# A gated local-attention kernel: another order for the first four tiles, two pairs of projection buffers, and other halves gated at the end

## The chip, the cores and the metric

The kernel runs on one core of a Trainium2 chip, in one launch. The metric is the device time of the launch in microseconds (us), the median of several runs. Five engines work side by side, each through its own queue in order: TensorE (PE, matrix products and transposes, with its weight loads listed as PEld), VectorE (DVE), ScalarE (ACT), GpSimd (POOL) and SyncE (SP), which here issues all DMA transfers. Where an engine needs what another one makes, it waits on a semaphore.

## The reference

`x` has 2048 rows (positions) of 640 numbers. It is normalised row by row; two branches start from the normalised rows, and the result is `x + s * g`:

```python
xn = _layernorm(x, axis=-1)                        # S = 2048 rows, D = 640
# branch A: 32 heads of 20, each position attends to 8 positions, 2 apart, backwards
qkv = xn @ wqkv                                    # D x 3D
logits = einsum(q, k at pos - 2*w for w in 0..7) * Dh ** -0.5    # masked before the start
s = (softmax(logits) applied to the gathered v) @ wo             # D x D
# branch B: bilinear feed-forward
g = silu(((xn @ w_gate) * (xn @ w_up)) @ w_down)   # D x 1536, D x 1536, 1536 x D
return x + s * g
```

## The kernel before

**Tiles.** The 2048 rows are cut into 16 tiles of 128. Tiles 0 to 7 hold the even positions, tiles 8 to 15 the odd ones, so that a neighbour two positions back lies in the same half. A tile is loaded (`load_x`, line 132), its mean and variance are taken on DVE (`moments`, L185 and L186), one over the root of the variance is formed by a square root on ACT (L191) and a few narrow DVE instructions (`rstd`, L194 to L206), and the tile is scaled in place by one DVE instruction (`apply`, L209). `norm` does the last two steps for `n` tiles.

**Products in three parts.** Each float32 factor is split into a rounded part `hi`, a copy made by ACT, and the remainder `lo`, a subtraction on DVE or POOL (`split`, L85 and L86). A product is then three matmuls: hi by hi, hi by lo and lo by hi, each over five blocks of 128 of the 640 columns (`KD = 5`), so 15 matmuls for one output.

**Transposes.** PE needs a tile with its columns on the partitions. `trans` (line 218) transposes the five blocks of tiles 0 to 7 on PE (L223) into two PSUM buffers of four blocks and one. ACT copies each buffer to the `hi` part (L224), and DVE subtracts to get the `lo` part (L225). Tiles 8 to 15 go through DVE's own transpose (`trans_odd`).

**Stages.** (1) The start, lines 628 to 704: loads, norms and transposes of the tiles, with the first products of the projection to q, k and v (`qkv`, line 281; group 0 of six groups of heads, 300 columns) and of the gate and up matrices (`gate_up`, `f` a block of 128 of the 1536 columns, `ch` a chunk of four tiles). (2) The bulk: for twelve units (a group of heads and a half of the positions) the projection, with the attention on DVE advanced a little at a time between products (`advance`), and the rest of the gate and up products. (3) The output projection of the 16 tiles (`out_proj`, line 469), stored to `s_scr`. (4) The down projection, 56 block products (`product`), whose results are gathered, sent through SiLU on ACT (L579) and gated and added (`gated`, L584 and L585) before the store.

**Order.** Everything is in the order in which the program text issues it, on each engine's queue (a manual schedule); a tile pool hands out buffers by tag in turn, and an instruction that takes a buffer waits until the last reader of that buffer is done. What matters for the change:

- `load_wq` loads the weights of group 0 in five slices of 128 rows, `split_wq` splits them (hi on ACT, lo on POOL); `load_wf` and `split_wf` do the same for a gate/up block. All of them use tag `wraw` with three buffers, so the fourth load waits until the first buffer has been split.
- A DMA takes one of eight semaphores in turn and, on SP, the DMA eight places further on waits for it to land.
- `gate_up_first` runs the gate and up products for the first two tiles alone (256 of 512 columns), and `gate_up(0, 0, part=part0)` finishes the other two.
- PSUM tag `q` has four buffers, shared by transposes, `qkv`, `idle_product` (products of the identity with itself, whose result is not used) and the output projection.
- `out_proj` writes each tile to a buffer of tag `gs` (two buffers) by two ACT copies (L476) and stores it from there.
- `halves` holds the subtractions that `trans_odd` has put off; `low_parts` issues them.

The start, as issued before:

```python
norm(0, 1)
mv1 = moments(1, 1)
split_wq(0, nc.gpsimd, (0, 3))
trans(0)
idle_product()
split_wq(0, nc.gpsimd, (3, KD))
load_x(12, 1, xa[:, 0:1])
norm(1, 1, mv1)
begin_unit(0, False)
mv2 = moments(2, 2)
qkv(0, 0, ((0, 0), (1, 0), (0, 1)))
trans(1)
```

Of the kernel before, what the change touches and what calls it, by code (L numbers as in the profile page):

```python
# [19 lines left out]
P = 128  # L20
# [30 lines left out]
def kernel(  # L51
# [48 lines left out]
    def load_wq(g, parts):  # L100
        c3 = 3 * GROUPS[g] * DH
        wq_raw[g] = []
        for p in parts:
            t = st([P, p[-1] - p[0], c3], "wraw", 3)
            for k0, k1 in zip(p, p[1:]):
                nc.sync.dma_start(t[:, k0 - p[0]:k1 - p[0]], wqkv[g][:, k0:k1, :])
                wq_raw[g].append((k0, k1, t[:, k0 - p[0]:k1 - p[0]]))
# [24 lines left out]
    def load_x(s, n, t, cuts=(0, D)):  # L132
        j = tile_column(s)
        for c0, c1 in zip(cuts, cuts[1:]):
            nc.sync.dma_start(t[:, :, c0:c1], (xbv if s < NE else xv)[:, j:j + DIL * (n - 1) + 1:DIL, c0:c1])
        for i in range(n):
            xt[s + i] = t[:, i, :]

    xa, xe = st([P, 3, D], "t", 2), st([P, 3, D], "t", 2)
    load_x(0, 1, xa[:, 0:1], (0, HALF, D))  # L140
    load_x(1, 1, xa[:, 1:2])
    load_wq(0, ((0, 1, 2, 3), (3, 4, 5)))
    load_x(2, 2, xe[:, 0:2])
    load_wf(0)
    load_wf(1)
    xc = st([P, NE, D], "xc", NCH)
    load_x(4, 4, xc[:, 0:4])
    load_x(8, 4, xc[:, 4:8])
    xd = st([P, 1, D], "o", 1)
# [60 lines left out]

    def norm(s0, n, mv=None):
        mv = moments(s0, n) if mv is None else mv
        r = st([P, n], "r", 2)
        rstd(mv[:, :, 1], r, n)
        for i in range(n):
            apply(xt[s0 + i], mv[:, i, 0:1], r[:, i:i + 1])

    def trans(s):
        hi, lo = xT_tile(s)
        for k0, k1 in ((0, 4), (4, KD)):  # L220
            p = pt([P, k1 - k0, P], "q", 4)
            for k in range(k0, k1):
                nc.tensor.transpose(p[:, k - k0, :], xt[s][:, k * P:(k + 1) * P], ident)  # L223
            nc.scalar.activation(hi[:, k0:k1, :], p, AF.Copy)  # L224
            nc.vector.tensor_sub(lo[:, k0:k1, :], p, hi[:, k0:k1, :].bitcast(F32))  # L225

# [15 lines left out]

    halves = []

    def trans_odd(s):
# [8 lines left out]
        halves.append(lambda: nc.vector.tensor_sub(lo, y, hi.bitcast(F32)))  # L254

    def low_parts():
        while halves:
            halves.pop(0)()

# [20 lines left out]

    def qkv(u, i, parts=ALL3):
        g, r = UN[u]
        c = GROUPS[g] * DH
        p = pt([P, 3 * c], "q", 4)
        hi, lo = xT[(r * NE + i) // TPC]
        t0 = (i % TPC) * P
        a, b = (hi[:, :, t0:t0 + P], lo[:, :, t0:t0 + P]), wq[g]
        mm3(p, [([t[:, k, :] for t in a], [t[:, k, :] for t in b]) for k in range(KD)], parts)
        nc.scalar.activation(kv_t[u][:, :, W - 1 + i, :], p[:, c:].rearrange("p (a c) -> p a c", a=2), AF.Copy)  # L289
        nc.scalar.activation(q_t[u][:, i, :], p[:, :c], AF.Copy)  # L290
        for i0, i1 in ((1, 5), (5, NE)):
            if i == i1 - 1:
                for p0, p1 in ((0, 112), (112, 127)):
                    nc.sync.dma_start(kv_t[u][p0 + 1:p1 + 1, :, i0 - 1:i1 - 1, :],
                                      kv_t[u][p0:p1, :, W - 1 + i0:W - 1 + i1, :])
# [122 lines left out]

    def gate_up_first(f, ch):

        pp = [pt([P, CH], "g", 2), pt([P, CH], "u", 2)]
        for parts, first in ((ALL3[:2], True), (ALL3[2:], False)):
            for n in range(2):
                gate_up_half(f, ch, n, pp[n], slice(0, CH // 2), parts=parts, first=first, last=not first)
        return pp

# [42 lines left out]
    def out_proj(s):  # L469
        a = oT.pop(s)  # L470
        y = st([P, D], "gs", 2)
        for n in range(2):
# [153 lines left out]


    norm(0, 1)
    mv1 = moments(1, 1)
    split_wq(0, nc.gpsimd, (0, 3))  # L630
    trans(0)
    idle_product()
    split_wq(0, nc.gpsimd, (3, KD))
    load_x(12, 1, xa[:, 0:1])
    norm(1, 1, mv1)
    begin_unit(0, False)
    mv2 = moments(2, 2)
    qkv(0, 0, ((0, 0), (1, 0), (0, 1)))
    trans(1)
    load_x(13, 1, xa[:, 1:2])  # L640
    split_wf(0, nc.gpsimd, range(KD + 1))
    norm(2, 2, mv2)
    qkv(0, 1)
    split_wf(1, nc.gpsimd, range(KD + 1))
    zero_front(0)
    part0 = gate_up_first(0, 0)
    trans(2)
    trans(3)
    mask = st([1, NE, W], "mask", 1)
# [6 lines left out]
    norm(4, 4)  # L656
    qkv(0, 2)
    qkv(0, 3)
    gate_up(0, 0, part=part0)
    trans(4)  # L660
    trans(5)
    moments(8, 2, mvo[:, 0:2])
    gate_up(1, 0, amid=(lambda: trans(6),))
    moments(10, 2, mvo[:, 2:4])
    load_xq(8, 4, xc[:, 4:8])
    trans(7)
    load_wf(2)
    qkv(0, 4)
# [126 lines left out]
    for m in range(n_prod):  # L795
# [10 lines left out]
        if j < 2 and n:  # L806
            gated(2 * n - 2 + j)
            load_sx(2 * n + j)
        if m == n_prod - 2:
            gated(NT - 2)  # L810
            gated(NT - 1, HALF)
    gated(NT - 1, 0)

# [42 lines left out]
```

## Time and profile before

| | us |
|---|---|
| median of 3 runs | 789.6 (789.08 to 789.82) |
| the profiled execution: its own time | 789.2 |
| its span, first to last instruction | 787.3 |
| PE busy | 778.0 (99%) |
| DVE busy | 658.7 (84%) |
| ACT busy | 234.6 (30%) |
| POOL busy | 147.8 (19%) |
| mean granted clock of PE | 0.999 |

The span is what the profiler sees from the first to the last instruction; the execution's own time is 1.9 us longer. Rows of a timeline give the start in us from the span's start, the duration in us, the engine, the line of the kernel, the operation, output and inputs by the program's names, the count of instructions joined in the row, and in brackets the time for which the engine stood idle before and what ended that wait. A row that joins several instructions runs from the first one's start to the last one's end. A matmul's end is modelled and overlaps the next one's start, so PE's pace is read from the distance between starts.

### The profile page before, as it was taken

What the parts mean: (1) busy time and instruction counts of PE and PEld (TensorE: products, weight loads), DVE (VectorE), ACT (ScalarE), POOL (GpSimd) and SP (SyncE); (2) the same over time, 40 slices, a digit from 0 to 9 for tenths busy, and PEclk for the clock granted to TensorE, in tenths of its full rate; (3) what the DMA queues carried; (4) which work ended last, traced back from release to release, by engine and by line L of the source; (5) the groups of instructions that cost most, each with busy time, mean ns of one, the idle gap of its engine ahead of it and who ended that gap; (6) DMA issues with size and microseconds to landing.
All of it is one profiled execution on the core that took longest, in us unless ns stands there. A gap on an engine that the chain in (4) does not pass through costs nothing. (4 is left out here: it accounts for less than half of the span.)

```text
span 787.3 us, 11221 instructions
## 1 busy us (share of the span) xinstructions
PE 778.0 (99%) x4456; PEld 708.8 (90%) x4456; DVE 658.7 (84%) x658; ACT 234.6 (30%) x536; POOL 147.8 (19%) x110
## 2 busy tenths in 40 slices
PE   8999999999999999999999999999999999999997
PEld 6989898889898888898898989888899999999997
DVE  6889899999999979997999999991277677777775
ACT  5324211121112211311221212113356554444442
POOL 6201212022013200500231000113377600000000
PEclk9999999999999999999999999999999999999999
DMA  8272122141132321404032222322796574555533
GB/s 315 73 229 81 36 69 64 48 123 48 49 94 80 94 71 61 118 27 112 28 118 72 62 82 72 107 87 66 182 258 201 181 262 133 204 200 186 181 101 135
DMA packets 81517, 92.68 MB, mean 118 GB/s; under 512 B 23016, under 2 KB 63032, under 8 KB 81336
## 3 DMA queue, kind: packets, MB, share of 16 engines
q1 hardware_dynamic: 81464, 91.96, 37.7%
q8 instruction: 35, 0.57, 0.3%
q14 instruction: 18, 0.15, 0.1%
HBM read 54.53 MB, written 28.31 MB: 105 GB/s over the span
## 5 line engine op out<-in xcount | busy, mean ns | idle before, releaser
L95 PE MATMUL u<-xc,wf 128*128 128x512 f32 (+1 forms) x735 | 176.2, 390 | 0.0
L95 PE MATMUL g<-xc,wf 128*128 128x512 f32 (+1 forms) x735 | 176.1, 390 | 0.0
L95 PEld LDWEIGHTS u<-xc,wf 128*128 128x128 f32 x735 | 135.7, 187 | 32.2
L95 PEld LDWEIGHTS g<-xc,wf 128*128 128x128 f32 x735 | 135.3, 187 | 31.0
L95 PE MATMUL q<-wqh,xc 128*128 128x300 f32 (+1 forms) x960 | 159.7, 309 | 1.8 <-ACT xc L224 1.0
L95 PEld LDWEIGHTS q<-wqh,xc 128*128 128x128 f32 x960 | 146.0, 188 | 4.3 <-ACT xc L224 1.9
L321 DVE TENSOR_TENSOR t<-q,kv 128x1600 f32<-128x1600 f32 (+1 forms) x48 | 99.3, 2069 | 9.6 <-DMA kv<-kv 9.6
L342 DVE TENSOR_TENSOR t<-e,kv 128x1600 f32<-128x1600 f32 (+1 forms) x48 | 97.5, 2051 | 1.1
L86 POOL TENSOR_TENSOR wf<-wraw,wf 128x256 fp32r<-128x256 f32 (+2 forms) x22 | 47.8, 2197 | 247.6 <-ACT wf L85 229.3
L324 DVE TENSOR_REDUCE lg<-t 128x80 f32<-128x1600 f32 (+1 forms) x48 | 92.6, 1930 | 1.2
L389 ACT ACTIVATE gs<-g 128x512 f32<-128x512 f32 x48 | 28.7, 598 | 205.9 <-PE g L95 197.1
L95 PE MATMUL q<-wql,xc 128*128 128x300 f32 (+1 forms) x480 | 86.0, 309 | 0.0
L350 DVE TENSOR_TENSOR t<-t,t 128x1600 f32<-128x1600 f32 (+1 forms) x36 | 78.0, 2166 | 1.1
L95 PEld LDWEIGHTS q<-wql,xc 128*128 128x128 f32 x480 | 74.3, 188 | 0.0
L289 ACT ACTIVATE kv<-q 128x200 f32<-128x200 f32 (+1 forms) x96 | 33.5, 349 | 133.5 <-PE q L95 133.5
L598 PE MATMUL q<-xc,wf 128*128 128x320 f32 x432 | 67.3, 309 | 0.0
L598 PEld LDWEIGHTS q<-xc,wf 128*128 128x128 f32 x432 | 64.3, 188 | 0.0
L86 POOL TENSOR_TENSOR wql<-wraw,wqh 128x300 fp32r<-128x300 f32 (+4 forms) x15 | 34.2, 2300 | 142.6 <-ACT wqh L85 142.6
L95 PE MATMUL q<-wf,wf 128*128 128x320 f32 x156 | 35.9, 312 | 0.6 <-ACT wf L85 0.6
L400 DVE TENSOR_TENSOR hs<-u,gs 128x512 f32<-128x512 f32 x39 | 26.6, 683 | 0.8 <-issue 0.8
L95 PEld LDWEIGHTS q<-wf,wf 128*128 128x128 f32 x156 | 26.0, 188 | 0.9 <-ACT wf L85 0.8
L86 DVE TENSOR_TENSOR wf<-ot,wf 128x640 fp32r<-128x640 f32 x13 | 13.6, 1045 | 14.1 <-ACT wf L85 14.1
(160 smaller groups left out, 891.4 us busy)
## 6 DMA issues: line engine op xcount, KB each, us to landing
h_scr<-hs SPq DMA_DIRECT2D x48, 256.0 KB, 2.3
wraw<-in_wgu SPq DMA_DIRECT2D x12, 640.0 KB, 4.8
t<-h_scr SPq DMA_DIRECT2D x8, 768.0 KB, 7.4
s_scr<-gs SPq DMA_DIRECT2D x16, 320.0 KB, 3.6
hs<-s_scr SPq DMA_DIRECT2D x16, 320.0 KB, 4.4
gs<-in_x SPq DMA_DIRECT2D x16, 320.0 KB, 4.7
out<-q SPq DMA_DIRECT2D x15, 320.0 KB, 2.5
wraw<-h_scr SPq DMA_DIRECT2D x12, 384.0 KB, 5.7
```

The source lines that it names most:

```text
L86: eng.tensor_sub(lo, raw, hi.bitcast(F32))
L95: nc.tensor.matmul(acc, a, b, start=first and n == 0, stop=last and n == len(runs) - 1)
L289: nc.scalar.activation(kv_t[u][:, :, W - 1 + i, :], p[:, c:].rearrange("p (a c) -> p a c", a=2), AF.Copy)
L321: nc.vector.tensor_mul(t, q.rearrange("p i c -> p (i c)").unsqueeze(1).to_broadcast([P, 2, NE * c]), places(0, j))
L324: nc.vector.tensor_reduce(out=lg[:, :, j:j + 2].rearrange("p n a -> p a n"), in_=heads(t), op=ALU.add, axis=AX.X)
L342: nc.vector.tensor_mul(heads(t), pw, heads(places(1, j)))
L350: nc.vector.tensor_add(acc, acc, t)
L389: nc.scalar.activation(gs, pp[0], AF.Copy)
L400: nc.vector.tensor_mul(hs, pp[1], gs)
L598: nc.tensor.matmul(p, y[:, i, k], wd_t[name][k][:, l], start=new and r == 0, stop=r == len(runs) - 1, skip_group_check=True)
```

## The change

It has four parts.

1. **Loads.** After tile 0 come the first three slices of group 0's weights, then tile 1, then the other two slices. Tiles 2 and 3 are loaded one at a time, and tiles 4 to 7 ahead of the second gate/up block.
2. **Start.** Tile 0 is scaled and transposed in two cuts, of two and three blocks. The subtractions for the `lo` parts of tiles 0 to 7 are put off into `halves` and issued by `low_parts` after the norm of the next tile (tiles 0 to 2) or right after the transposes. Tiles 2 and 3 get moments and norm one by one. The 15 matmuls of the first `qkv` run in another order, with tile 1's transposes ahead of the last two. `gate_up_first` begins with hi by hi alone; between its four parts stand tile 2's transposes, low parts, tile 3's norm and tile 2's `qkv`, then tile 3's transposes, then tile 3's low parts. The split of the second gate/up block moves behind that.
3. **Output projection.** Odd tiles below 12 are written to the two buffers of tag `hs`, the others to the two of tag `gs`.
4. **End.** Of the last two tiles, both high halves are gated after product 53 of 0 to 55, tile 14's low half after product 54, and tile 15's low half after product 55, as before.

```diff
--- before.py
+++ after.py
@@ -99,7 +99,7 @@
 
     def load_wq(g, parts):
         c3 = 3 * GROUPS[g] * DH
-        wq_raw[g] = []
+        wq_raw.setdefault(g, [])
         for p in parts:
             t = st([P, p[-1] - p[0], c3], "wraw", 3)
             for k0, k1 in zip(p, p[1:]):
@@ -138,13 +138,15 @@
 
     xa, xe = st([P, 3, D], "t", 2), st([P, 3, D], "t", 2)
     load_x(0, 1, xa[:, 0:1], (0, HALF, D))
+    load_wq(0, ((0, 1, 2, 3),))
     load_x(1, 1, xa[:, 1:2])
-    load_wq(0, ((0, 1, 2, 3), (3, 4, 5)))
-    load_x(2, 2, xe[:, 0:2])
+    load_wq(0, ((3, 4, 5),))
+    load_x(2, 1, xe[:, 0:1])
+    load_x(3, 1, xe[:, 1:2])
     load_wf(0)
-    load_wf(1)
     xc = st([P, NE, D], "xc", NCH)
     load_x(4, 4, xc[:, 0:4])
+    load_wf(1)
     load_x(8, 4, xc[:, 4:8])
     xd = st([P, 1, D], "o", 1)
     load_x(14, 1, xa[:, 2:3])
@@ -208,21 +210,30 @@
     def apply(y, m, r):
         nc.vector.tensor_scalar(y, y, m, r, op0=ALU.subtract, op1=ALU.mult)
 
-    def norm(s0, n, mv=None):
+    def norm(s0, n, mv=None, cuts=(0, D)):
         mv = moments(s0, n) if mv is None else mv
         r = st([P, n], "r", 2)
         rstd(mv[:, :, 1], r, n)
         for i in range(n):
-            apply(xt[s0 + i], mv[:, i, 0:1], r[:, i:i + 1])
-
-    def trans(s):
+            for c0, c1 in zip(cuts, cuts[1:]):
+                apply(xt[s0 + i][:, c0:c1], mv[:, i, 0:1], r[:, i:i + 1])
+
+    halves = []
+
+    def low_parts():
+        while halves:
+            halves.pop(0)()
+
+    def trans(s, cuts=(0, 4, KD)):
+
         hi, lo = xT_tile(s)
-        for k0, k1 in ((0, 4), (4, KD)):
+        for k0, k1 in zip(cuts, cuts[1:]):
             p = pt([P, k1 - k0, P], "q", 4)
             for k in range(k0, k1):
                 nc.tensor.transpose(p[:, k - k0, :], xt[s][:, k * P:(k + 1) * P], ident)
             nc.scalar.activation(hi[:, k0:k1, :], p, AF.Copy)
-            nc.vector.tensor_sub(lo[:, k0:k1, :], p, hi[:, k0:k1, :].bitcast(F32))
+            halves.append(lambda p=p, k0=k0, k1=k1: nc.vector.tensor_sub(lo[:, k0:k1, :], p,
+                                                                         hi[:, k0:k1, :].bitcast(F32)))
 
 
 
@@ -239,8 +250,6 @@
         for a in range(NQ):
             nc.tensor.matmul(p[:, a], sel[:, a], mro, start=True, stop=True)
         nc.scalar.activation(mrq, p, AF.Copy)
-
-    halves = []
 
     def trans_odd(s):
         for a in range(NQ):
@@ -253,10 +262,6 @@
         low_parts()
         halves.append(lambda: nc.vector.tensor_sub(lo, y, hi.bitcast(F32)))
 
-    def low_parts():
-        while halves:
-            halves.pop(0)()
-
 
     UN = [(g, r) for g in range(len(GROUPS)) for r in range(DIL)]
     q_t, kv_t, kv_buf, kv_zero = {}, {}, {}, {}
@@ -278,14 +283,19 @@
             nc.gpsimd.memset(kv_t[u][0:1, :, 0:W - 1, :], 0.0)
             kv_zero[r] = GROUPS[g]
 
-    def qkv(u, i, parts=ALL3):
+    ALL_RUNS = [(a, b, k) for a, b in ALL3 for k in range(KD)]
+
+    def qkv(u, i, runs=ALL_RUNS, amid=None):
+
         g, r = UN[u]
         c = GROUPS[g] * DH
         p = pt([P, 3 * c], "q", 4)
-        hi, lo = xT[(r * NE + i) // TPC]
         t0 = (i % TPC) * P
-        a, b = (hi[:, :, t0:t0 + P], lo[:, :, t0:t0 + P]), wq[g]
-        mm3(p, [([t[:, k, :] for t in a], [t[:, k, :] for t in b]) for k in range(KD)], parts)
+        for n, (a, b, k) in enumerate(runs):
+            if amid is not None and n == amid[0]:
+                amid[1]()
+            nc.tensor.matmul(p, xT[(r * NE + i) // TPC][a][:, k, t0:t0 + P], wq[g][b][:, k], start=n == 0,
+                             stop=n == len(runs) - 1, skip_group_check=amid is not None)
         nc.scalar.activation(kv_t[u][:, :, W - 1 + i, :], p[:, c:].rearrange("p (a c) -> p a c", a=2), AF.Copy)
         nc.scalar.activation(q_t[u][:, i, :], p[:, :c], AF.Copy)
         for i0, i1 in ((1, 5), (5, NE)):
@@ -416,12 +426,14 @@
         while unfinished:
             unfinished.pop(0)()
 
-    def gate_up_first(f, ch):
+    def gate_up_first(f, ch, between):
 
         pp = [pt([P, CH], "g", 2), pt([P, CH], "u", 2)]
-        for parts, first in ((ALL3[:2], True), (ALL3[2:], False)):
+        for parts, first in ((ALL3[:1], True), (ALL3[1:], False)):
             for n in range(2):
                 gate_up_half(f, ch, n, pp[n], slice(0, CH // 2), parts=parts, first=first, last=not first)
+                if not first or n:
+                    between.pop(0)()
         return pp
 
 
@@ -468,7 +480,7 @@
 
     def out_proj(s):
         a = oT.pop(s)
-        y = st([P, D], "gs", 2)
+        y = st([P, D], "hs" if s % 2 and s < NT - 4 else "gs", 2)
         for n in range(2):
             c = slice(n * HALF, (n + 1) * HALF)
             p = pt([P, HALF], "q", 4)
@@ -625,27 +637,35 @@
         return lambda: None
 
 
-    norm(0, 1)
+    norm(0, 1, cuts=(0, 2 * P, D))
     mv1 = moments(1, 1)
-    split_wq(0, nc.gpsimd, (0, 3))
-    trans(0)
+    split_wq(0, nc.gpsimd, (0, 2))
+    trans(0, (0, 2, KD))
     idle_product()
-    split_wq(0, nc.gpsimd, (3, KD))
+    norm(1, 1, mv1)
+    split_wq(0, nc.gpsimd, (2, KD))
     load_x(12, 1, xa[:, 0:1])
-    norm(1, 1, mv1)
+    low_parts()
+    mv2 = moments(2, 1)
     begin_unit(0, False)
-    mv2 = moments(2, 2)
-    qkv(0, 0, ((0, 0), (1, 0), (0, 1)))
-    trans(1)
+    hh, hl, lh = ([(a, b, k) for k in range(KD)] for a, b in ((0, 0), (0, 1), (1, 0)))
+    qkv(0, 0, hh[:3] + hl[:3] + lh[:3] + hh[3:] + lh[3:] + hl[3:], (13, lambda: trans(1)))
     load_x(13, 1, xa[:, 1:2])
+    low_parts()
+    norm(2, 1, mv2)
     split_wf(0, nc.gpsimd, range(KD + 1))
-    norm(2, 2, mv2)
-    qkv(0, 1)
+    mv3 = moments(3, 1)
+    qkv(0, 1, hh + hl + lh)
+
+    def second():
+        trans(2)
+        low_parts()
+        norm(3, 1, mv3)
+        qkv(0, 2)
+
+    part0 = gate_up_first(0, 0, [second, lambda: trans(3), low_parts])
     split_wf(1, nc.gpsimd, range(KD + 1))
     zero_front(0)
-    part0 = gate_up_first(0, 0)
-    trans(2)
-    trans(3)
     mask = st([1, NE, W], "mask", 1)
     nc.gpsimd.memset(mask, 0.0)
     for i in range(NE - 1):
@@ -654,16 +674,18 @@
     nc.gpsimd.tensor_copy(sel.rearrange("p q (b i) -> p q b i", i=QB),
                           ident.rearrange("p (q i) -> p q i", i=QB).unsqueeze(2).to_broadcast([P, NQ, NQ, QB]))
     norm(4, 4)
-    qkv(0, 2)
     qkv(0, 3)
     gate_up(0, 0, part=part0)
     trans(4)
+    low_parts()
     trans(5)
+    low_parts()
     moments(8, 2, mvo[:, 0:2])
-    gate_up(1, 0, amid=(lambda: trans(6),))
+    gate_up(1, 0, amid=(lambda: trans(6), low_parts))
     moments(10, 2, mvo[:, 2:4])
     load_xq(8, 4, xc[:, 4:8])
     trans(7)
+    low_parts()
     load_wf(2)
     qkv(0, 4)
     qkv(0, 5)
@@ -806,9 +828,11 @@
         if j < 2 and n:
             gated(2 * n - 2 + j)
             load_sx(2 * n + j)
-        if m == n_prod - 2:
-            gated(NT - 2)
+        if m == n_prod - 3:
+            gated(NT - 2, HALF)
             gated(NT - 1, HALF)
+        elif m == n_prod - 2:
+            gated(NT - 2, 0)
     gated(NT - 1, 0)
```

## The prediction

> **What bounds the kernel now.** I read the page first, then stretches of the span, then TensorE's timeline, then those of the engines that release it. The page's engine rows:
>
> ```profile
> PE 778.0 (99%) x4456; PEld 708.8 (90%) x4456; DVE 658.7 (84%) x658; ACT 234.6 (30%) x536; POOL 147.8 (19%) x110
> ```
>
> TensorE (PE) is busy for 778.0 of 787.3 us, and the edits add or drop no product. So only its 9.3 us of idle time can change. The stretches say where that lies (first number after the colon: PE's busy time):
>
> ```profile
> 0.00:28.00 28.00, 24.33 (x155) 20.64 (x156) 20.63 (x66) 12.75 (x38) 14.44 (x31) 1.00 0.73 262
> ...
> 782.00:787.30 5.30, 0.24 (x2) 0.00 (x0) 2.14 (x5) 0.44 (x1) 0.00 (x0) 0.90 0.35 125
> ```
>
> 3.7 us are idle in the first 28 us and 5.1 after the last product. Between them the table shows PE full, but for 0.55 us in 589 to 591. The change touches all three places. PE at the start (start, duration, and in brackets the idle time before it):
>
> ```profile
> 8.12 1.94 PE L95 MATMUL q<-wqh,xc 128*128 128x300 f32 x10 [0.46 <-ACT xc L224]
> ...
> 10.79 0.74 PE L223 MATMUL q<-ident,t 128*128 128x128 f32 x5
> 12.11 0.96 PE L95 MATMUL q<-wqh,xc 128*128 128x300 f32 x5 [0.58 <-ACT xc L224]
> ...
> 27.55 1.25 PE L223 MATMUL q<-ident,xc 128*128 128x128 f32 x10
> ```
>
> 8.12 is the first product of tile 0, 10.79 tile 1's transposes, 12.11 tile 1's products, 27.55 the transposes of tile 4, before which nothing waits. After 27.55 the order on PE is the same in both kernels, so the start is judged by one number: when PE reaches tile 4. VectorE (DVE):
>
> ```profile
> 10.08 0.61 DVE L209 TENSOR_SCALAR t<-t,mv,r 128x640 f32<-128x640 f32 x1
> ...
> 15.42 2.03 DVE L209 TENSOR_SCALAR t<-t,mv,r 128x640 f32<-128x640 f32 x2
> ...
> 20.66 0.88 DVE L185 BATCH_NORM_STATS2 stats<-xc 128x6 f32<-128x320 f32 x2
> ...
> 26.20 2.18 DVE L209 TENSOR_SCALAR xc<-xc,mv,r 128x640 f32<-128x640 f32 x4
> ```
>
> From the first statistics of tile 4 (20.66) to its scaled rows (first of the four at 26.20, 0.61 long) DVE needs 6.15 us, 6.2 to PE's start. Before, that ended at 26.9, 0.65 ahead of PE.
>
> **Start, step by step** (times on the old clock).
>
> *First product.* The scaling of tile 0 is cut at two of five blocks (0.61 x 2/5 = 0.25 before the transposes may start), and only two blocks are copied before the first product. That puts it at 7.2, behind the one idle product that follows the transposes, not 8.12.
>
> *Tile 1.* This gain isn't kept. ScalarE (ACT) now has tile 1's square root ahead of the copy of the third weight slice, and that root needs tile 1's moments, so tile 1's landing. Its load now stands behind three slices:
>
> ```profile
> 7.13 0.45 ACT L85 ACTIVATE wqh<-wraw 128x300 fp32r<-128x300 f32 x1 [0.53 <-DMA wraw<-in_wqkv]
> ```
>
> The third slice came at 7.1, after both halves of tile 0, tile 1 and two slices. The same bytes now end with tile 1 instead. From issue: two halves and three slices at 0.44 to 0.47 each from 0.75 put it at 3.0, and with 3.4 to landing (320 KB) or 3.9 (a slice), 6.4 to 6.9. I take 7.0; ends 6.1 (DVE is not free earlier) and 7.5. Then: statistics and aggregate 1.15 (6.09 to 7.21 before), root 0.29, third slice copied 0.45, its low part on GpSimd (POOL) 0.83, so PE has two products at 7.2, the third at 9.0, the low weights at 9.8. On DVE: root to scaled rows took 8.81 to 10.69, so 8.2 to 10.05. Only behind that stand the low parts of tile 0, which used to run at 8.10 (0.89 for both): now to 10.95. PE needs them for three products, then four more, so tile 1's transposes start at 11.7 (10.79 before) and its products, 1.31 later as before, at 13.0. That is 0.9 behind 12.11.
>
> *Tiles 2 and 3.* The old PE ran 15.44 from 12.11 to 27.55. New: tile 1's 15 products 2.18, ten gate/up halves at 0.117 = 1.17, transposes of tile 2 to its products 1.31 (nothing stands between them, so the 0.76 that PE waited at 19.8 stays), products 2.16, ten halves 1.17: tile 3's transposes at 13.0 + 8.0 = 21.0. Then DVE decides. Tile 3's copy is ready 1.25 later (0.65, then the copy 0.60), its two low parts take 0.85, and only behind them stand the statistics of tile 4, from 23.1 instead of 20.66. Plus 6.2: tile 4's transposes at 29.3. PE itself has 0.46 + 1.17 + 2.06 + 3.51 = 7.2 after 21.0 and would be there at 28.2: a new wait of 1.1. Start: 29.3 - 27.55 = +1.8.
>
> *Unknown: DVE beside POOL.* The two L209 at 15.42 took 1.02 each with POOL splitting weights, the four at 26.20 0.55 each with POOL idle, but the one at 10.08 took 0.61 though POOL was busy to 10.3. Tile 1's scaling now has three POOL splits beside it: 0 to +0.47. I take +0.2, nearer to the row of the same tile. Start: +2.0, from +0.9 (tile 1 by 6.1, no meeting) to +2.8.
>
> *Moved loads.* Tiles 4 to 7 are issued ahead of the second gate/up weights, so by 14.5 to 18, both early enough for 23. Those weights wait for POOL's third split (9.8, formerly 8.5), with tile 8's load behind them on SP; the queue holds 1.3 MB until then, so no gap arises. Statistics of tiles 8 to 15 are wanted from 30: nothing. Their low parts on POOL end near 27, wanted at 31.
>
> **Projection buffers.** A waits view of 575 to 600:
>
> ```profile
> ACT gs L476 <- DMA s_scr<-gs: 3.4, 1, 3.4
> ...
> PE q L95 <- ACT wf L85: 0.6, 1, 0.6
> ```
>
> ACT stood 3.4 us for a `gs` buffer until 577.31; the copy of the next tile (579.40), DVE's sums and, at 589.30, the copy that PE waited for came late in that chain. The gap there is 0.86 where 0.15 is usual: 0.71 lost. With odd tiles in `hs` a buffer comes back after four tiles, so ACT goes on at 574.0, and at 576.2 with the second half: at least 1.4 earlier, more than the 0.71 that is needed. `hs` must be free of the last h store (issued 566.06, landing 2.3 later, wanted 570.2), and the two `hs` of tile 14 (copied at 623.06) of the stores of tiles 9 and 11 (evacuated at 616.87, 3.6 to landing). Both hold. I take -0.7; ends 0 and -0.7.
>
> **End.**
>
> ```profile
> 780.67 0.82 DVE L584 TENSOR_TENSOR q<-q,hs 128x640 f32<-128x640 f32 x1 [0.54 <-ACT q L579]
> ...
> 783.72 0.49 DVE L585 TENSOR_TENSOR q<-q,gs 128x320 f32<-128x320 f32 x1
> ```
>
> After the last SiLU (782.28 + 0.44) DVE still has tile 14's add, tile 15's high half and its low half, to 784.21. New: both high halves go between 777.6 and 779.65, beside the last two products, and tile 14's low half at 780.7 to 781.7. Then 782.75 to 783.77 is left: -0.44. The high half of 15 needs its `gs` load (issued at 773.83, 4.7 to landing = 778.5, wanted 779.2); half a microsecond later it would push L621 and take most of this back. Ends 0 and -0.5.
>
> **Sum.** +2.0 - 0.7 - 0.45 = +0.85. The profiled execution took 789.2 (span 787.3 and 1.9 around it), 0.4 under the median of 789.6. From the median: 790.5.
>
> **Rivals.**
>
> *VectorE and GpSimd collide (slower).* Both L209 runs on the new path, tile 1's beside the weight splits and tile 4's beside GpSimd's later splits and copies, cost 1.02 instead of 0.55. Start 1.8 + 0.5 + 0.5 = 2.8, net +1.65: 791.3. For it the 15.42 row, against it 10.08. It decides once both collide in full. Chance 0.21. [...]
>
> *Tile 1 lands by 6.1.* Start +0.9 to +1.0, net -0.2: 789.4. For: 6.4 from issue; against: 7.13 for the same bytes. 0.15.
>
> *The buffers don't cure 589.* The chain there also holds weight loads and sums slowed to 1.16. +0.7: 791.2. 0.09.
>
> *VectorE keeps up (faster).* If the statistics of tiles 4 to 7 did not come late and tile 1 came by 6.1, PE would have 27.0, start -0.5, net -1.7: 787.9. The 6.2 us of DVE rows speak against it. 0.06.
>
> *The clock falls.* PE would pause about 1.5 us after two products, longer than any pause in the rows after 6 us (PEclk stayed 1.00). One stretch of 3.4 us at half the rate would lose 1.7: 792.2. 0.05. [...] The trace's own cold stretch (idle products 0.64 apart until 4.7, then 0.32) is as long: 1.37 to 4.7, 3.3 us.
>
> **Numbers.** The forecast has 0.44, own range 789.9 to 791.1. 0.2% (1.6 us) is about what a measurement of this kernel can tell from no change: bounds 788.0 and 791.2. Slower: collision 0.21, clock 0.05, half of the 589 case 0.05, the forecast's own upper edge 0.05 = 0.36. Faster 0.07. Same 0.57. The range 789.0 to 791.9 takes in the forecast, the collision, the early landing and the uncured stall, and leaves out clock and faster case.
>
> **What would show it.** Right: first product near 7.2, a pause of over 1 us after two of them, tile 1's products near 13, PE waiting for L209's successor about 1 us before tile 4's transposes near 29.3; no PE gap near 589 + 2; last DVE end 1.5 us after PE's last product instead of 2. Wrong: tile 4's transposes by 27.5, or two or more new waits after them.

## The result: 791.2 us against 789.3, a dearer start, a cheaper middle and end

| | us | runs |
|---|---|---|
| before, measured again beside it | 789.33 | 9 (789.08 to 790.04) |
| after | 791.2 | 9 (790.75 to 794.78) |
| ratio | 1.0030, 95% interval 1.0018 to 1.0042 | |

The changed kernel is slower by 0.3% (the ratio is that of the means, 791.8 and 789.4; the medians give 0.24%). The profiled execution of it is the slowest of the nine (794.78, span 792.9), so its rows have to be sorted into what other executions show too and what only this one does. The line numbers in its rows are those of the changed kernel: L211 scales a tile, L187 takes its statistics, L196 to L208 form one over the root, L233 transposes, L234 and L235 make the high and low parts, L297 is the projection, L95 the gate and up products, L86 a weight split, L413 the multiplication of a finished gate and up product. First the engine row of the page:

```profile
PE 780.7 (98%) x4456; PEld 710.0 (90%) x4456; DVE 670.1 (85%) x662; ACT 234.7 (30%) x537; POOL 146.9 (19%) x110
```

and some stretches of its span. After the length stand the busy times of PE, PEld, DVE, ACT and POOL, each with its count of instructions, then the granted clock, the share of DMA and its GB/s:

```profile
0.00:28.00 28.00, 24.01 (x147) 19.93 (x148) 19.48 (x61) 12.21 (x38) 13.79 (x28) 1.00 0.73 262
28.00:32.00 4.00, 1.98 (x17) 1.60 (x16) 3.86 (x8) 1.94 (x5) 2.23 (x6) 1.00 0.04 11
32.00:36.00 4.00, 4.00 (x13) 3.18 (x12) 3.83 (x11) 0.77 (x2) 0.00 (x0) 0.57 0.19 55
...
380.00:390.00 10.00, 9.07 (x39) 7.01 (x38) 10.00 (x5) 1.58 (x2) 4.42 (x2) 1.00 0.09 27
...
575.00:600.00 25.00, 25.00 (x172) 25.00 (x171) 17.53 (x22) 14.57 (x35) 16.72 (x17) 1.00 0.93 250
```

PE is full from 575 to 600, where before it was idle for 0.55:

```profile
575.00:600.00 25.00, 24.45 (x165) 24.08 (x165) 18.31 (x23) 15.09 (x37) 19.12 (x19) 1.00 0.80 222
```

It now stands idle for 2.0 of the 4 us from 28 to 32. In the next 4 us it is busy throughout, but at a mean clock of 0.57, and between 380 and 390 there is an idle 0.93 that before did not have. PE's timeline at the start:

```profile
8.08 0.73 PE L297 MATMUL q<-wqh,xc 128*128 128x300 f32 x2
...
11.90 0.71 PE L233 MATMUL q<-ident,t 128*128 128x128 f32 x5
...
13.18 0.96 PE L297 MATMUL q<-wqh,xc 128*128 128x300 f32 x5 [0.30 <-ACT xc L234]
...
21.15 0.71 PE L233 MATMUL q<-ident,t 128*128 128x128 f32 x5
...
29.86 0.74 PE L233 MATMUL q<-ident,xc 128*128 128x128 f32 x5 [1.23 <-issue]
31.38 0.74 PE L233 MATMUL q<-ident,xc 128*128 128x128 f32 x5 [0.78 <-DVE xc L211]
31.87 5.28 PE L95 MATMUL g<-xc,wf 128*128 128x512 f32 x15
```

PE is 1.07 behind from tile 1's products on (13.18 against 12.11); the last three rows are the rest of the loss. Tile 4's transposes wait 1.23 and come at 29.86 (27.55 before). Tile 5's, which before followed in the same row, wait another 0.78. The 15 gate products behind them take 5.28 instead of 3.75. DVE and GpSimd show why the two waits are there. DVE:

```profile
5.57 1.69 DVE L211 TENSOR_SCALAR t<-t,mv,r 128x256 f32<-128x256 f32 x2
...
23.23 0.88 DVE L187 BATCH_NORM_STATS2 stats<-xc 128x6 f32<-128x320 f32 x2
...
27.36 0.32 DVE L196 TENSOR_SCALAR rstd<-mv 128x4 f32<-128x4 f32 x1
...
28.16 0.54 DVE L206 TENSOR_TENSOR rstd<-rstd 128x4 f32<-128x4 f32 x1
...
29.14 3.13 DVE L211 TENSOR_SCALAR xc<-xc,mv,r 128x640 f32<-128x640 f32 x4
```

GpSimd, beside those rows:

```profile
5.39 1.66 POOL L86 TENSOR_TENSOR wql<-wraw,wqh 128x300 fp32r<-128x300 f32 x2 [4.07 <-ACT wqh L85]
...
28.08 0.60 POOL L674 COPY sel<-ident 128x512 f32<-128x512 f32 x1
29.33 1.54 POOL L413 TENSOR_TENSOR hs<-hs,gs 128x512 f32<-128x512 f32 x1 [0.65 <-ACT hs L412]
```

before, at the same places:

```profile
24.80 0.17 DVE L194 TENSOR_SCALAR rstd<-mv 128x4 f32<-128x4 f32 x1
25.60 0.16 DVE L204 TENSOR_TENSOR rstd<-rstd 128x4 f32<-128x4 f32 x1
...
28.42 1.29 POOL L403 TENSOR_TENSOR hs<-hs,gs 128x512 f32<-128x512 f32 x1 [6.12 <-ACT hs L402]
28.87 1.68 DVE L225 TENSOR_TENSOR xc<-q,xc 128x512 fp32r<-128x512 f32 x4 [0.48 <-ACT xc L224]
```

and the line of the scaling by itself (count: shortest, median and longest duration in ns):

```profile
L211 DVE TENSOR_SCALAR xc<-xc,mv,r x4: 602/608/1558, 29.1 to 31.7; 128x640 f32<-128x640 f32 x4
```

Three of the four scalings took 0.60 to 0.61; the one of tile 5, begun while GpSimd's multiplication ran, took 1.56 and ended 0.35 after it. Before, that multiplication ran beside DVE's low parts (28.42 and 28.87), and both took what they took apart: 0.69 for four blocks at 28.87 and at 33.41, 1.29 for the multiplication there and at 37.06. The statistics of tile 4 start at 23.23, and from there to its scaling stand 5.91 us instead of 5.54 in before: the narrow rows at 27.36 and 28.16, 0.17 and 0.16 long in before, met GpSimd's memset (26.39, 1.26 long) and copy. At the end of the kernel the rows on DVE are

```profile
789.08 0.49 DVE L596 TENSOR_TENSOR q<-q,hs 128x320 f32<-128x320 f32 x1 [1.05 <-ACT q L591]
789.60 0.49 DVE L597 TENSOR_TENSOR q<-q,gs 128x320 f32<-128x320 f32 x1
```

the last ending 1.52 after PE's last product (788.57), where before it was 1.97.

All that follows uses one table by stages, worked out from the timelines: when the gate products behind tile 5's transposes start, the time from there to the end of PE's last product, from that to DVE's last end, and from that to the end of the span. Profiles with the same start lie up to 0.6 apart in the first column: 28.47 to 29.03 with the old start, 31.87 to 32.37 with the new one, where tile 1 landed at 6.50 in the earliest and at 7.63 in the latest of them.

| | gate products start | to PE's last end | to DVE's last end | to the span's end |
|---|---|---|---|---|
| before | 28.56 | 753.69 | 1.97 | 3.10 |
| after, first profile | 31.87 | 756.70 | 1.52 | 2.81 |
| after, second profile (below) | 32.19 | 752.73 | 1.52 | 2.82 |

So what the two profiles have in common is +3.3 to +3.6 at the start, -0.95 in the middle and -0.45 at the end; the last column gives another -0.3, which is not put down to a part, since it lies between 2.64 and 3.10 in the three profiles with the old end. For the second profile that is 3.6 - 0.95 - 0.45 - 0.3 = +1.9, and 789.3 + 1.9 = 791.2. The 4.0 that the first profile has more in the middle are the gate products at the low clock (5.28 - 3.75 = 1.53) and two waits of PE, 0.93 at 386 and 0.94 at 444. Read from start to start, each of the two puts PE 1.2 further behind the second profile; the idle time is shorter, because the modelled end of a product lies behind the start of the next.

### The profile page after: what moved, and what is told of

It is laid out like the page before. It is cut to its first block, busy times and chain, and to the rows that moved or that the text cites. A ratio compares the mean times of both kernels' runs of the same rounds, so it can differ in the third digit from the quotient of the medians.

```text
span 792.9 us, 11231 instructions
## 1 busy us (share of the span) xinstructions
PE 780.7 (98%) x4456; PEld 710.0 (90%) x4456; DVE 670.1 (85%) x662; ACT 234.7 (30%) x537; POOL 146.9 (19%) x110
## 4 chain that ended last, share of the span: by engine, by line
PE 53%; DVE 36%; issue 7%; DMA 2%; ACT 1%; SPq 0%; DVEq 0%; POOL 0%; ACTq 0%; POOLq 0%
PE q L610 11%; DVE t L331 9%; PE q L95 9%; PE g L95 9%; DVE t L352 8%; PE u L95 8%; PE q L297 7%; DVE t L360 7%; PE u L610 5%; DVE lg L334 4%; PE g L610 3%; DVE hs L410 2%; DMA kv<-kv 1%; DVE o L363 1%; DMA h_scr<-hs 1%
## 5 line engine op out<-in xcount | busy, mean ns | idle before, releaser
L95 PE MATMUL g<-xc,wf 128*128 128x512 f32 (+1 forms) x735 | 177.6, 393 | 0.0
L95 PE MATMUL u<-xc,wf 128*128 128x512 f32 (+1 forms) x735 | 176.5, 391 | 0.9 <-DVE hs L410 0.9
L95 PEld LDWEIGHTS u<-xc,wf 128*128 128x128 f32 x735 | 135.6, 187 | 33.6 <-DVE hs L410 1.6
L95 PEld LDWEIGHTS g<-xc,wf 128*128 128x128 f32 x735 | 136.5, 189 | 31.4
L297 PE MATMUL q<-wqh,xc 128*128 128x300 f32 (+1 forms) x960 | 160.7, 310 | 2.3 <-ACT q L300 0.9
L297 PEld LDWEIGHTS q<-wqh,xc 128*128 128x128 f32 x960 | 146.1, 188 | 5.2 <-ACT q L300 1.5
L331 DVE TENSOR_TENSOR t<-q,kv 128x1600 f32<-128x1600 f32 (+1 forms) x48 | 101.4, 2113 | 10.5 <-DMA kv<-kv 10.5
L352 DVE TENSOR_TENSOR t<-e,kv 128x1600 f32<-128x1600 f32 (+1 forms) x48 | 99.8, 2098 | 1.1
L86 POOL TENSOR_TENSOR wf<-wraw,wf 128x256 fp32r<-128x256 f32 (+2 forms) x22 | 46.7, 2141 | 260.2 <-ACT wf L85 260.2
L297 PE MATMUL q<-wql,xc 128*128 128x300 f32 (+1 forms) x480 | 86.5, 310 | 0.2 <-POOL wql L86 0.2
L360 DVE TENSOR_TENSOR t<-t,t 128x1600 f32<-128x1600 f32 (+1 forms) x36 | 81.8, 2272 | 1.1
L297 PEld LDWEIGHTS q<-wql,xc 128*128 128x128 f32 x480 | 74.4, 188 | 0.5 <-POOL wql L86 0.5
L86 POOL TENSOR_TENSOR wql<-wraw,wqh 128x300 fp32r<-128x300 f32 (+4 forms) x15 | 34.5, 2324 | 144.5 <-ACT wqh L85 144.5
L95 PE MATMUL q<-wf,wf 128*128 128x320 f32 x156 | 35.7, 310 | 0.0
L86 DVE TENSOR_TENSOR wf<-ot,wf 128x640 fp32r<-128x640 f32 x13 | 16.2, 1245 | 12.3 <-ACT wf L85 12.3
L95 PEld LDWEIGHTS q<-wf,wf 128*128 128x128 f32 x156 | 26.1, 188 | 0.0
```

Of the source, the lines that this page charges most:

```text
L86: eng.tensor_sub(lo, raw, hi.bitcast(F32))
L95: nc.tensor.matmul(acc, a, b, start=first and n == 0, stop=last and n == len(runs) - 1)
L297: nc.tensor.matmul(p, xT[(r * NE + i) // TPC][a][:, k, t0:t0 + P], wq[g][b][:, k], start=n == 0, stop=n == len(runs) - 1, skip_group_check ...
L331: nc.vector.tensor_mul(t, q.rearrange("p i c -> p (i c)").unsqueeze(1).to_broadcast([P, 2, NE * c]), places(0, j))
L352: nc.vector.tensor_mul(heads(t), pw, heads(places(1, j)))
L360: nc.vector.tensor_add(acc, acc, t)
```

## Experiments: the parts one by one

**The start alone.**

```diff
-        y = st([P, D], "hs" if s % 2 and s < NT - 4 else "gs", 2)
+        y = st([P, D], "gs", 2)
...
-        if m == n_prod - 3:
-            gated(NT - 2, HALF)
-            gated(NT - 1, HALF)
-        elif m == n_prod - 2:
-            gated(NT - 2, 0)
+        if m == n_prod - 2:
+            gated(NT - 2)
+            gated(NT - 1, HALF)
```

> The changed kernel with the projection's buffers and the end as before, so that only the other start is left. Theory (the parts add up, and the start is dearer than predicted): the two traces put the start at +2.3 at tile 4's transposes (29.86 against 27.55) and +0.8 at tile 5's, 3.1 in all, and about 1.7 more in an execution whose granted clock falls to one half for 3.4 us. Median 789.3 + 3.1 = 792.4, and up to 794.1 where the clock falls. Rival (the prediction's own sum): start +2.0, 791.3. In the profile the theory wants a PE wait before tile 4's transposes and a second one, on L211, before tile 5's; the rival has only the first.

Measured: 793.96 (792.83 to 794.73), ratio 1.0049 (1.0033 to 1.0065), 3.9 us, 1.6 above the 792.4 of the theory. Its timeline on PE has both waits again:

```profile
30.36 0.73 PE L233 MATMUL q<-ident,xc 128*128 128x128 f32 x5 [1.24 <-issue]
31.87 0.74 PE L233 MATMUL q<-ident,xc 128*128 128x128 f32 x5 [0.78 <-DVE xc L211]
```

Stages: 32.37, 753.80, 1.97. The start is 0.5 later than in the first profile of the changed kernel because tile 1 landed later: DVE waited 0.81 for it and began its statistics at 7.65 (7.19 there), and the square root on ACT, the copy of the third weight slice behind that, and PE's products came 0.5 later with it. So the start is 3 to 4 us dearer, not 2.0; middle and end are those of before. The profiled execution, 792.97, is 1.0 below the median; what the slower ones lose beyond it no profile shows.

**The projection's buffers alone**, **the end alone**, and **both**, each on the kernel before:

```diff
-        y = st([P, D], "gs", 2)
+        y = st([P, D], "hs" if s % 2 and s < NT - 4 else "gs", 2)
```

> The kernel before with odd tiles of the output projection in hs. Theory: PE's gap at 589 goes, -0.7 to -0.9: 788.5, and in the profile PE has no gap of more than 0.2 between 575 and 600. Rival (the gap is DVE's and the weight loads', not the buffers'): the gap stays or moves, and the time is 789.3.

Measured: 788.22 (787.80 to 791.19), ratio 0.9983 (0.9972 to 0.9993). Stages 28.64, 752.75, 1.97: the middle is 0.94 shorter, and PE is busy for all of the 25 us between 575 and 600.

```diff
-        if m == n_prod - 2:
-            gated(NT - 2)
-            gated(NT - 1, HALF)
+        if m == n_prod - 3:
+            gated(NT - 2, HALF)
+            gated(NT - 1, HALF)
+        elif m == n_prod - 2:
+            gated(NT - 2, 0)
```

> The kernel before with the other halves gated at the end. Theory: DVE's last instruction ends 1.5 us after PE's last product instead of 2.0, so -0.45: 788.9. Rival (the last store, not DVE's end, decides, or the earlier halves push L621 back): 789.3.

Measured: 789.0 (788.37 to 791.54), ratio 0.9990 (0.9979 to 1.0000). The time alone hardly tells this from nothing; the stages do: 28.47, 753.75, and 1.53 instead of 1.97.

> The kernel before with both of these and its own start. Theory (the two parts are independent): 789.3 - 0.7 - 0.45 = 788.2, faster than both kernels. Rival (they share a cover: the buffers only bring forward what then waits at the end): 788.9 or more.

Measured: 787.83 (787.24 to 788.43), ratio 0.9974 (0.9965 to 0.9984), the lowest ratio of all kernels here. Stages 29.03, 752.75, 1.53: the two gains add up. This is the version that beats both: the kernel before with the two late parts and its own start.

## Experiments: what makes the start dear

**Tile 1's load first.**

```diff
+    load_x(1, 1, xa[:, 1:2])
     load_wq(0, ((0, 1, 2, 3),))
-    load_x(1, 1, xa[:, 1:2])
```

> The changed kernel with tile 1's load ahead of the first three weight slices, as it was before. Theory (the order of loads costs the start its first 1.0: the slices come earlier, GpSimd's first split then runs beside the second cut of tile 0's scaling, which takes 1.1 instead of 0.4, and tile 1's statistics start at 7.2 instead of 6.1): tile 1's products come about 1.0 earlier and all behind them with them: 790.0. Rival (the third slice is what tile 0 and tile 1 wait for in either order): its copy comes 0.7 later, and the time stays 790.8 to 791.2.

Measured: 790.05, ratio 1.0011 (1.0002 to 1.0020), 1.1 below the changed kernel's 791.1 to 791.2 (ratios 1.0024 and 1.0030). DVE and GpSimd:

```profile
5.59 0.80 DVE L211 TENSOR_SCALAR t<-t,mv,r 128x256 f32<-128x256 f32 x2
...
6.34 1.64 POOL L86 TENSOR_TENSOR wql<-wraw,wqh 128x300 fp32r<-128x300 f32 x2 [5.02 <-ACT wqh L85]
```

GpSimd's first split now starts when both cuts of tile 0's scaling are nearly over, and they take 0.80 together instead of 1.69. The first product comes at 7.20 and tile 1's at 12.30, 0.9 earlier each; both waits at tiles 4 and 5 stay (1.27 and 0.78), as all ahead of them came earlier alike. So the new order of loads costs 1 us. It does so in two ways. In the first profile tile 1 landed at 6.50 and DVE was busy with tile 0 until 7.19. In the second, in that of the start alone and in three more with this order of loads tile 1 landed only at 7.24 to 7.63, and its statistics began 0.02 after that. With tile 1 first it landed at 5.38.

**GpSimd's work later.**

```diff
-        if not running:
+        if not running and not put_off:
             finish_piece()
...
     split_wf(1, nc.gpsimd, range(KD + 1))
+    norm(4, 4)
+    qkv(0, 3)
+    gate_up(0, 0, part=part0, put_off=True)
...
+    gate_up(1, 0, amid=(lambda: trans(6), low_parts))
     zero_front(0)
     mask = st([1, NE, W], "mask", 1)
...
-    norm(4, 4)
-    qkv(0, 3)
-    gate_up(0, 0, part=part0)
...
```

The multiplication of the first gate and up product is issued with the next one, and the memsets and copies on GpSimd (`zero_front`, `mask`, the selector) come behind it in the program.

> The changed kernel with the work on GpSimd that ran beside the scaling of tiles 4 to 7 (the fronts, mask and selector, and the first gate product's multiplication) issued behind the next gate product. Theory (the chance meeting of DVE and GpSimd costs 0.55 ahead of tile 4 and the 0.78 before tile 5): L211 takes 0.55 each instead of 0.78, T4 at 29.3, no wait at T5, -1.3: 789.7, and the clock falls more seldom. Rival (the four rows are slow for another reason): they stay 0.78 each, 791.0 to 791.2.

Measured: 789.65, ratio 1.0012 (1.0002 to 1.0021). DVE:

```profile
28.90 0.17 DVE L196 TENSOR_SCALAR rstd<-mv 128x4 f32<-128x4 f32 x1
...
30.30 2.19 DVE L211 TENSOR_SCALAR xc<-xc,mv,r 128x640 f32<-128x640 f32 x4
```

The narrow rows are 0.16 to 0.18 again, the four scalings 2.19 instead of 3.13; PE's wait before tile 4 falls from 1.23 to 0.86, by the 0.37 of the narrow rows, and the one before tile 5 is gone. The theory's 789.7 holds.

**Statistics early.**

```diff
+    mv4 = st([P, 4, 2], "mv4", 1)
...
         norm(3, 1, mv3)
+        moments(4, 2, mv4[:, 0:2])
...
-    norm(4, 4)
+    moments(6, 2, mv4[:, 2:4])
+    norm(4, 4, mv4)
```

> The changed kernel with the statistics of tiles 4 and 5 issued behind tile 3's scaling, where DVE stands idle for 2.2 us before tile 3's low parts, instead of behind those. Theory (the late statistics hold back tile 4): the chain comes 2.0 earlier, PE waits neither before tile 4's transposes (1.23) nor before tile 5's (0.78), so -2.0 and no fall of the clock: 791.0 - 2.0 = 789.0. Rival (GpSimd's work beside DVE holds it back): the earlier scaling meets the memset and the copy on GpSimd, costs about 1.0 each, and half of the pauses stays: 790.0.

Measured: 790.21, ratio 1.0015 (1.0007 to 1.0024), the rival's number. DVE and PE:

```profile
27.17 0.97 DVE L207 TENSOR_SCALAR rstd<-rstd 128x4 f32<-128x4 f32 x1
...
28.38 3.66 DVE L211 TENSOR_SCALAR xc<-xc,mv,r 128x640 f32<-128x640 f32 x4
...
29.60 1.30 PE L233 MATMUL q<-ident,xc 128*128 128x128 f32 x10 [0.49 <-PE u L95]
```

The statistics end earlier as meant, and the chain behind them runs into more of GpSimd's work: a row of 0.17 takes 0.97, the four scalings 3.66. Half of the gain is lost again; of the waits, 0.49 before tile 4 stays.

**All three cures at once.** Its diff is the three above.

> The changed kernel with the three cures at once: tile 1's load ahead of the slices, the statistics of tiles 4 and 5 early, GpSimd's work later. Theory (the three causes are all of the new start's loss): -1.0 for the load, -1.25 and -0.78 for the two pauses: 791.0 - 3.0 = 788.0, which is that of the kernel before with the two late parts alone (787.8); T4 near 27.7 with no wait. Rival (something else in the new start costs too): a wait at T4 is left and the time is 789.0 or more.

Measured: 788.32 (788.22 to 788.66), ratio 0.9989 (0.9980 to 0.9997). PE and DVE:

```profile
27.65 1.25 PE L233 MATMUL q<-ident,xc 128*128 128x128 f32 x10
...
26.27 2.18 DVE L211 TENSOR_SCALAR xc<-xc,mv,r 128x640 f32<-128x640 f32 x4
```

There is no wait before tile 4 or 5; the gate products start at 28.66, 0.1 behind before. So, within the 0.6 by which equal starts differ, the three causes are the whole of the start's loss. The time is 0.3 above the theory's; the middle, 753.80, is 1.1 longer than in the second profile of the changed kernel (see the last section).

**And tile 2's transposes one product earlier.**

```diff
-                if not first or n:
-                    between.pop(0)()
+                between.pop(0)()
...
-    part0 = gate_up_first(0, 0, [second, lambda: trans(3), low_parts])
+    part0 = gate_up_first(0, 0, [lambda: trans(2), second, lambda: trans(3), low_parts])
```

> The same with tile 2's transposes issued between the first gate and the first up product instead of behind both, so that the up product (0.6) runs while ScalarE copies them. Theory: the wait of 0.58 ahead of tile 2's products goes, and PE, which decides here, gets to tile 4 0.5 earlier: 787.5, below every kernel so far. Rival (DVE decides again: the statistics and scaling of tile 4 come no earlier): 788.0.

Measured: 788.1 (787.88 to 789.21), ratio 0.9985 (0.9976 to 0.9994). The wait of 0.58 is gone and the gate products start at 28.27, 0.39 earlier, so PE and not DVE decided there; the theory's 787.5 was not reached. The times of the two kernels are too near to each other to tell apart, and neither has a lower ratio than the kernel with the two late parts alone.

## Experiments: the clock

**The changed kernel again.**

> The changed kernel once more, on the chip of its three companions. Theory (the clock falls for one stretch of 3.41 us when that stretch, counted from the start of the clock's first full stretch, holds enough of the two pauses): two groups of runs again, near 791.0 and near 792.2, the upper one with the lower mean clock, and in the profile the stretch falls only if both pauses (1.23 and 0.78) lie in the stretch before it. Rival (the first measurement was disturbed): one group, 790.5 or 791.2, and no fall.

Measured: 791.12 (790.79 to 791.95), ratio 1.0024 (1.0015 to 1.0034). The second group near 792.2 did not show; one run, 791.95, has the lower mean clock of 0.997. The theory's place for the stretches holds in the four profiles that have both pauses. From 4.92 us on, the granted clock of the first profile changes only at steps of 3.413 us: it is 1.0 for 27.31 us (8 steps), 0.5 for one step, and 1.0 again for 757.76 us (222 steps); in before it is 1.0 for 781.65 us (229 steps). These are the stretches around tile 4's waits in the first profile:

```profile
28.81:32.22 3.41, 1.58 (x12) 1.36 (x13) 3.34 (x7) 1.39 (x4) 1.54 (x1) 1.00 0.11 32
32.22:35.63 3.41, 3.41 (x10) 2.67 (x9) 3.38 (x10) 0.58 (x2) 0.00 (x0) 0.50 0.15 45
```

and in the second, where the steps lie 1.65 later:

```profile
27.05:30.46 3.41, 2.16 (x20) 1.98 (x19) 3.10 (x10) 1.75 (x5) 2.72 (x11) 1.00 0.00 0
30.46:33.88 3.42, 2.64 (x17) 2.14 (x15) 3.42 (x6) 1.53 (x4) 0.74 (x1) 1.00 0.25 77
33.88:37.29 3.41, 3.41 (x19) 2.79 (x18) 2.52 (x9) 0.88 (x3) 0.00 (x0) 1.00 0.00 0
```

The waits are the same, but a step's edge at 30.46 lies between them, no stretch has PE idle for more than 1.25, and the clock stays at 1.0. In the profiles of the start alone and of tile 1's load first the edge also falls between the two (at 30.58 and 29.2), PE is busy for 2.17 and 2.63 of the stretches beside it in the one and 2.13 and 2.62 in the other, and the clock stays at 1.0 there too.

**The pauses filled.** First four idle products ahead of tile 4's transposes and two ahead of tile 5's (`idle_products(n)` issues `n` of them), then half as many, 2 and 1:

```diff
+    idle_products(4)
     trans(4)
     low_parts()
+    idle_products(2)
     trans(5)
```

> The changed kernel with four idle products ahead of tile 4's transposes and two ahead of tile 5's, which fill PE's two pauses (1.23 and 0.78) and leave what PE waits for as it is. Theory: the pauses let the granted clock fall to one half for one stretch of 3.41 us in some of the executions (those at 792.0 to 792.5 against 790.75 to 791.2). The idle products leave T4 near 29.9 and T5 near 31.4, the clock stays 1.0 behind them, and no run has the 1.2: all near 791.0. Rival (the clock's fall is not caused by the pauses): the profile or some of the runs still show it, with about every second run at 792 or more.

Measured: 792.48 (792.41 to 792.6), ratio 1.0042 (1.0029 to 1.0055). One idle product is two rows of 0.32, so four overfill the pause: tile 4's transposes at 31.22, the gate products at 33.52, 1.3 later than in the second profile of the changed kernel, which is the whole difference in time. The expectation of times was wrong by that; the clock did not fall, and the five runs lie within 0.2.

> The changed kernel with half as many idle products in PE's two pauses: two ahead of tile 4's transposes (2 x 0.64 = 1.28 against a pause of 1.23), one ahead of tile 5's (0.64 against 0.78). Theory: nothing is held back (T4 and T5 within 0.1 of the changed kernel), and without pauses the clock does not fall: all runs near 791.0, none near 792.2. Rival (an idle product costs the path what it fills): 791.6 or more; or, if the pauses do not cause the fall, two groups as in the changed kernel.

Measured: 791.0 (790.82 to 791.28, and one at 793.2), ratio 1.0022 (1.0013 to 1.0030). Tile 4 comes at 29.92 and tile 5 at 31.44, there is no fall, and the run at 793.2 has a mean clock of 1.0, so it is something else. Filling costs nothing here and gains nothing in the median. That the pauses make the clock fall is likely by these runs but not shown: without filling, two runs of nine and one of nine had the lower mean clock of 0.997; with filling, none of five and none of eleven.

What is not settled is how little work makes the clock fall. The profile of the kernel with GpSimd's work later shows a fall at another place:

```profile
8.24:11.65 3.41, 2.30 (x10) 1.33 (x9) 3.03 (x11) 1.46 (x5) 2.26 (x3) 1.00 1.00 395
11.65:15.06 3.41, 3.41 (x14) 3.05 (x14) 1.39 (x5) 1.29 (x6) 0.39 (x1) 0.50 1.04 416
```

Here PE was busy for 2.30 of the stretch before, more than the 2.16 after which the clock did not fall above. So PE's busy time alone does not decide it, and the cause stays open. Nor is it shown whether transposes count like products: they are all but 0.35 of the 1.58 in the first profile.

## Why the prediction was right or wrong

The number, 790.5, was 0.7 short, within its range; its likeliest case, no change that can be told, was narrowly missed (0.24% by the medians, 0.18% to 0.42% by the interval). What happened is the first rival, VectorE and GpSimd colliding, at 791.3. That its number came within 0.1 is in part luck. Of the rows that it named tile 1's scaling lost nothing (0.63 at 9.61), and beside tile 4's it was the narrow rows and tile 5's scaling that were held up; its start of +2.8 was 0.5 to 0.8 too small, and the rest of its sum was too dear by about as much.

- **First product**: wrong. 7.2 was predicted and 8.08 came. The step that failed is "0.25 before the transposes may start": the two cuts took 1.69, since the weight slices that were moved forward also moved GpSimd's first split forward, onto them. With that undone (tile 1's load first) the product came at 7.20.
- **Tile 1**: transposes 11.90 (11.7 predicted), products 13.18 (13.0). The times were right. The reason, the load's landing at 7.0, holds in five of seven profiles with this order of loads (7.24 to 7.63); in the first the tile landed at 6.50 and was late because DVE was, until 7.19.
- **Tiles 2 and 3**: right. Tile 3's transposes 21.15 (21.0), statistics of tile 4 at 23.23 (23.1). The wait of 1.23 (1.1) is near in part by luck, as 0.37 of it comes from the collision named next and 0.86 is left without that.
- **Unknown, DVE beside POOL**: mis-sized, and the main error. +0.2 was taken, +1.0 was the upper end, and 1.4 was measured: 0.37 in the narrow rows ahead of tile 4, which were not thought of, and 1.0 behind it, the wait of 0.78 before tile 5 and what it drains. The row chosen as the nearest, 0.61 at 10.08, does not speak against a collision: GpSimd's instruction beside it ended 0.20 after the row's start, and only that tail was met.
- **Projection buffers**: the mechanism was right, the size too small, -0.95 measured for -0.7 (its own end): PE's start after the gap comes 0.74 earlier, the products behind it close up by another 0.11, and 0.08 is gained just ahead. **End**: right, -0.45 for -0.45. **Moved loads**: right but for the split that came with them.
- **The clock falls** (0.05, +1.7): it did in the first profile, for 1.53 (5.28 - 3.75), but behind tile 4's waits. At the place that was named, the pause after the first two products, it fell in the profile with GpSimd's work later. No row of before shows its stretch of 3.4 us at half the rate, only one of 3.3 us at the start; both falls lasted 3.41 us at a granted clock of 0.50. That a pause of 1.5 us sets off a fall is not shown: PE was busy for 1.58 of the 3.41 before the fall in the first profile, where no pause was longer than 1.23, and for 2.30 of the 3.41 before the other, where the longest was 0.60.
- **Sum**: +3.6 - 0.95 - 0.45 - 0.3 = +1.9 in the second profile, where +2.0 - 0.7 - 0.45 = +0.85 was predicted; the -0.3, between DVE's last end and the span's, was no term of it. Of the listed signs of an error, "two or more new waits after them" shows in the first profile (0.78, 0.93 and 0.94); the second has only the one of 0.78.

## What to carry to other kernels

When a step is moved on DVE, lay its new place beside GpSimd's timeline row by row, and follow the collision to the next tiles in the queue, not to the first alone; and when loads are moved, ask which work on a third engine they set off earlier. Test the parts of a change one by one: here two of four were sound and the other two hid them. Where time differs little, compare stages of the traces: the middle stage held to 0.1 us in seven profiles, where the times of one kernel scattered by 1.

## What was not expected of the hardware

In these traces a scaling or a narrow row on DVE that is held up by an instruction on GpSimd does not run slower throughout but ends a fixed time after it. In the first profile GpSimd's multiplication at 29.33 took 1.54 instead of 1.29, as it came behind tile 4's scaling, and tile 5's scaling then ended 0.35 after it. A scaling of 640 columns that is held up ends 0.35 after GpSimd's instruction, however long the two ran side by side: tile 1's (0.63 long), tile 2's (1.05) and tile 5's (1.56) alike, and both rows at 15.42 in before. The two cuts of tile 0, of 256 and 384 columns, end 0.15 and 0.22 after it, and the two narrow rows 0.02 and 0.03. So in these rows what a meeting cost was set by how much of the other instruction was left. Statistics (0.48 each) and the subtraction with one input in PSUM (0.69 for four blocks) took the same beside GpSimd as without.

The waits near 386 and 444 of the first profile go back to the same thing. Of the first:

```profile
381.93 4.12 DVE L331 TENSOR_TENSOR t<-q,kv 128x1920 f32<-128x1920 f32 x1
...
381.06 2.98 POOL L86 TENSOR_TENSOR wf<-wraw,wf 128x1280 fp32r<-128x1280 f32 x1 [41.04 <-ACT wf L85]
...
386.71 1.66 PE L95 MATMUL u<-xc,wf 128*128 128x512 f32 x6 [0.93 <-DVE hs L410]
```

A multiplication of 2.15 took 4.12 beside a split, and PE waited for DVE. Ahead of 444 another took 3.54 (at 431.39) beside the split at 429.95; there PE waited for ACT, whose copies stood behind an exponential that waited for DVE. In before the multiplication at 374.13 began 1.8 ahead of the split and took 2.15, and the split 3.23; in the second profile the split came 0.9 behind it, and it was the split that took longer, 4.08 instead of 2.98. So in each of these four meetings the one that began later was the one that took longer. What sets that order was not tried.

The three kernels with early statistics have one more buffer, of 32 bytes in each partition. Their middle stage took 753.40, 753.80 and 753.43; in the seven undisturbed profiles with paired buffers and without it, 752.70 to 752.79. PE has no gap there that would account for it. Behind 40 us, products of 300 columns start 138.3 ns apart on average in these three and 137.5 to 137.7 in all other profiles; over some 870 such distances that is 0.5 to 0.7 us of the 0.6 to 1.1 that the middle is longer. Whether the buffer does this, and what the rest is, was not tried.
